# Score products as 32x64 array tiles, and ninety small products in TensorE's warm-up

## The chip, the core and the metric

One core of one Trainium2 chip runs the whole program. The metric is the device time of one execution in microseconds (us); the median of three runs is compared. [...]

## The reference, cut to what matters

Three parts run one after another: a chunked linear attention with decay (4 batches, 8 heads, 768 positions, head size 32, state size 16), a gated feed-forward (width 256 to 1024 to 256), and a second feed-forward (256 to 2048 to 256). Only the attention's scores are touched by the change:

```python
L = np.exp(cum[:, :, :, None] - cum[:, :, None, :]) * causal
CB = np.einsum('bhin,bhjn->bhij', Cc, Bc)          # the scores
M = CB * L
y_intra = np.einsum('bhij,bhjd->bhid', M, xc)
y_inter = np.einsum('bhin,bhnd->bhid', Cc, state) * decay_to_i[:, :, :, None]
state = decay_full[:, :, None, None] * state + np.sum(Bx, axis=2)
...
k = np.maximum(xk @ w_k, 0.0); v = k * k @ w_v     # first feed-forward, gated by a sigmoid
...
g = h - np.tanh(h); out = g @ w_out                # second feed-forward
```

## The kernel before, in words

The attention works in 12 groups of 256 tokens (`NG`), three to a batch; a group has four chunks of 64 tokens (`NC4`, `L`), and all eight heads lie in the 128 partitions, 32 partitions (two heads of 16 states) to a quarter. For group k TensorE computes:

- `decays(k)`, pd: the exponents of the decay matrix, two 128x128 products (L427 for the first two groups, in f32; L431 later, in f32r);
- `scores(k)`, pcb (L475): for each chunk, both halves `jh` of its 64 keys and four quarters q, one f32 product with 32 partitions in, 32 out and 128 columns. That is 32 products in the program; the trace has each f32 product as two weight loads and two matmuls, so 64 of each;
- `inter(k)`, py (L485): 32 products (24 for a batch's first group) of 32 in, 32 out, 64 columns; `terms(k)`, py (L500): the state's increments; `intra(k)`, py (L507): 32 products with 64 in, 32 out.

`visit_a(j)` issues `scores(j+1)` and then `inter(j)`; `visit_b(j)` issues `terms(j+1)` and `intra(j)`. pc (L405, and L676 for group 0) is the sum that ScalarE turns into the scales `er`. The first feed-forward is written as pk, pr and acc products (L771 to L774, L781 to L783): six 512-column products to a half tile; the second as ph and acc products of the same lines.

The order of each engine's instructions comes in two parts. The prologue is the list `START`, written out by hand: a name stands for a piece of work, and `qz` clears the operand `quiet`, `wa` is a number of idle 128x128x512 bf16 products on it that only keep TensorE busy (L218), `ps` is the group-0 scales' product (L676), `d0`, `d1` the first decays, `p0` `scores(0)`, `v0` the whole first visit. `wa` stands ahead of all else on TensorE. The dictionary `fns` also has entries `wb`, `wc`, `wd`, which `START` does not name. All that follows is ordered by `Plan.run`, a list scheduler in the program text that gives each piece a planned cost (P is TensorE, A ScalarE, V VectorE) and picks the next by rank and planned start. So a changed cost in one call of `put` can move pieces on every engine. Engines work strictly in this order.

Of the kernel before, what the change touches and what calls it, by code (L numbers as in the profile page):

```python
# [16 lines left out]
P = 128  # L17
NB, NH, S, HD, NS = 4, 8, 768, 32, 16
NQ = NH // 2
L = 64  # L20
# [6 lines left out]
NC4 = GT // L  # L27
NGB = S // GT
NG = NTOK // GT
# [28 lines left out]


START = """  # L60
    qz tab Da Dla Dca Db0 Dx0 Db1 Dx1 W Db2 Dnk Dnr seg mk wa c0t c1t c0b st mk2 tri
    cA lA cC lC sA ss h0s x0a cD lD x0b ps pe d0 e0 dec dexp still heads c1b x1a x1b sD cum p0 s0 w0 m0 ob u0 h0 w1
    r0t r0b r1t r1b spread v0 d1 e1 pr0 nu
""".split()
# [6 lines left out]
def t_act(n, more=0.0):  # L71
    return 0.172 + n / 1200 + more
# [124 lines left out]
def chain_kernel(ctx, tc, xb, a, an, a0, bc, mu_k, mu_r, w_k, w_v, w_r, w_in, w_out, out):  # L197
    nc = tc.nc
    V, A, G, PE = nc.vector, nc.scalar, nc.gpsimd, nc.tensor
# [15 lines left out]
    def fill(n):  # L215

        for _ in range(n):
            PE.matmul(acc[:, 0], quiet, quiet.unsqueeze(1).to_broadcast([P, NC4, P]), start=True, stop=True)  # L218

    def bank(name, shape=(2, BLK)):  # L220
        return pairs.tile([P, *shape], F32, tag="pair", name=name)


    acc = accp.tile([P, 2, BLK], F32, name="acc")
# [14 lines left out]
    quiet = const.tile([P, P], BF16, name="quiet")  # L239
# [134 lines left out]
    xbt, bct, cp, bp, mt, sts, er = {}, {}, {}, {}, {}, {}, {}  # L374
# [9 lines left out]
    def apart(k):  # L384
        return bct[k][:, GT:].rearrange("p (e c i) -> p e c i", e=2, c=NC4)
# [73 lines left out]
    def quarter(q):  # L459
        return slice(32 * q, 32 * q + 32)  # L460

    def half(h):
        return slice(L * h, L * h + L)

    QUADS = [(q, q >> 1, q & 1) for q in range(4)]

    def scores(k):
        pcb = pcbs[k] = bank("pcb")
        pv = pcb.rearrange("p g (e c i) -> p g e c i", e=2, c=NC4)
        for c in range(NC4):  # L470
            for jh in range(2):
                o = L * c + 32 * jh
                for q, h2, hp in QUADS:
                    r = quarter(q)
                    PE.matmul(pv[quarter(2 * h2 + jh), hp, :, c], bct[k][r, o:o + 32], apart(k)[r, :, c], start=c == 0, stop=c == NC4 - 1, skip_group_check=True)  # L475

    def out_bank(k):
        pys[k] = bank("py")

    def inter(k):  # L480
        for c in range(0 if k % NGB else 1, NC4):
            for e in range(2):
                for q, h2, hp in QUADS:
                    r, o = quarter(q), quarter(2 * hp + e)
                    PE.matmul(  # L485
                        pys[k][o, h2 ^ hp, c * L:(c + 1) * L], sts[k][r, c, e * HD:(e + 1) * HD], cp[k][r, e, c * L:(c + 1) * L],
                        start=first(k, h2 ^ hp, 2 * hp + e), stop=False, skip_group_check=True,
                    )
# [28 lines left out]
    def visit_a(k):  # L517
        if k + 1 < NG:
            scores(k + 1)
        out_bank(k)  # L520
        inter(k)
# [32 lines left out]
    def prologue(fetch1):  # L554

        t0, t1, t2, t3, t4 = vec("f"), vec("h"), vec("s"), vec("l", F32R), vec("f")
        seg, one = t0[:, 0, 0:GT], t0[:, 1, 0:P]
        la, ca = t4[:, 0, 0:NU], t4[:NC, 1, 0:GT]
        tri, cf = t1[:, 0, 0:P], t3[:NC, :, 0:GT]
        ad, mk = t2[CUM:P, 0, 0:GT], t2[:, 1]  # L560
# [4 lines left out]
        st = early["st"] = held[:, 0, 0:GT].rearrange("p (k h j) -> p k h j", k=2, h=2)  # L565
# [4 lines left out]
        def warm(n):  # L570
            return lambda: fill(n)

        def load(t, v):
            return lambda: nc.sync.dma_start(out=t, in_=v)
# [33 lines left out]
        def causal(out, e):  # L608
            return lambda: copy(e, out[0:L], mk[0:L, 0:L].unsqueeze(1).to_broadcast([L, CQ, L]))
# [71 lines left out]
        def t_nu():  # L681
# [4 lines left out]
            G.memset(xall[:, :, 0:NB * (S + 1)].rearrange("p c (b s) -> p c b s", b=NB)[..., 0:1], 0.0)  # L686

        fns = dict(
            qz=lambda: V.memset(quiet, 0.0), wa=warm(8), wb=warm(3), wc=warm(2), wd=warm(2), seg=t_seg,
            mk=t_mk, mk2=t_mk2, st=t_st, tri=t_tri, still=t_still, heads=t_heads, spread=t_spread,  # L690
            tab=lambda: A.preload_act_table_set("natural_log_exp_and_others"),
            c0t=causal(by[0], "V"), c1t=causal(by[1], "V"), c0b=spread(by[0], CUM, TOK, soon, "A"), c1b=spread(by[1], CUM, TOK, soon, "A"),
# [3 lines left out]
            Da=load(ad, a0), Dla=load(la, a), Dca=load(ca, an), Dnk=load(mus["k"], mu_k), Dnr=load(mus["r"], mu_r), W=fetch1,  # L696
            Db0=lambda: bc_load(0), Db1=lambda: bc_load(1), Db2=lambda: bc_load(2), Dx0=lambda: xb_load(0), Dx1=lambda: xb_load(1),
# [12 lines left out]
    def attention():  # L710

        D, E, MK, CH, GS, BPt, X, XL, BL, PSX, PS = ({} for _ in range(11))
        users = []

        def put(*args, **kw):
            t = add(*args, **kw)
            users.append(t)
            return t

        def at(k):  # L720
            return RANK_T * k

        def scales(b, lo, rank, after):
            take = [(R["pair"], ("pc", b))] + ([(R["er"], b)] if b else [])
            p = put(dict(P=0.36), lambda e: scales_sum(b, lo), after, rank, take)
            PSX[b] = put(dict(A=t_act(S - lo)), lambda e: scales_exp(b, lo), [p], rank, uses=[take[0], (R["er"], b)], func="exp")
            return p

        PS[0] = scales(0, 2 * GT, at(2) - 2, [])
        X[0] = put(dict(A=t_act(BLK), V=t_dve(BLK)), lambda e: group_out(0, e), [], at(0), (), [(R["pair"], ("py", 0))])  # L730
        first_half = visited = None
        for k in range(1, NG + 1):
            if 2 <= k < NG:
                XL[k] = put(dict(S=0.47), lambda e, k=k: xb_load(k), [], at(k - 1.5), [(R["xb"], k)], dma=1.7)
                if k >= 3:
                    BL[k] = put(dict(S=0.47), lambda e, k=k: bc_load(k), [], at(k - 1.8), [(R["bc"], k)], dma=1.7)
                rw = put(dict(S=0.9), lambda e, k=k: rows(k), [], at(k - 1.2), [(R["rows"], k)], dma=0.2)
                D[k] = put(dict(P=0.47), lambda e, k=k: decays(k), [rw], at(k) - 1.5, [(R["pair"], ("pd", k)), (R["L"], k)], [(R["rows"], k)])
                E[k] = put(dict(A=t_act(1024)), lambda e, k=k: decays_exp(k), [D[k]], at(k) - 1.5, (), [(R["pair"], ("pd", k)), (R["L"], k)], func="exp")
                BPt[k] = put(dict(V=t_dve(GT)), lambda e, k=k: weigh(k), [XL[k]], at(k) - 1.5, [(R["bp"], k)], [(R["xb"], k)], port=True)  # L740
            b, g = divmod(k, NGB)
            if g == 0 and k < NG:
                pr = put(dict(S=0.45), lambda e, b=b: prep_rows(b), [PS.get(b - 2)], at(k - 1.2), (), dma=0.2)
                PS[b] = scales(b, 0, at(k) - 1.7, [pr])
            if k >= 2:
                j = k - 1
                take = ([(R["pair"], ("pcb", k))] if k < NG else []) + [(R["pair"], ("py", j))]
                use_a = [(R["cp"], j), (R["state"], j), (R["bc"], k)]
                use_b = [(R["pair"], ("py", j)), (R["L"], j), (R["xb"], j), (R["bp"], k), (R["xb"], k)]
                first_half = put(dict(P=1.85 if k < NG else 0.85), lambda e, j=j: visit_a(j), [CH[j], GS[j], BL.get(k), D.get(k), PS.get(b) if k < NG else None, MK[j]], at(j), take, use_a)  # L750
                pause = put(dict(X=PAUSE), lambda e: None, [first_half])
                visited = put(dict(P=1.25 if k < NG else 0.75), lambda e, j=j: visit_b(j), [pause, XL.get(j), XL.get(k), BPt.get(k)], at(j), (), use_b)
                X[j] = put(dict(A=t_act(BLK), V=t_dve(BLK)), lambda e, j=j: group_out(j, e), [visited], at(j), (), [(R["pair"], ("py", j))])
            if k == NG:
                break
            MK[k] = put(dict(V=t_dve(1024)), lambda e, k=k: mask(k), [first_half, E.get(k)], at(k), (), [(R["pair"], ("pcb", k)), (R["L"], k)])
            CH[k] = put(
                dict(V=0.29 * moves(k)), lambda e, k=k: chain(k), [visited, PSX[b] if k > 1 else None], at(k) - 0.5,
                ([] if g else [(R["state"], k)]) + ([(R["state"], k + 1)] if g < NGB - 1 else []),
                [(R["pair"], ("py", k - 1)), (R["er"], b)] + ([(R["state"], k)] if g else []), port=True,  # L760
            )
            GS[k] = put(dict(V=t_dve(BLK)), lambda e, k=k: group_scale(k), [BL.get(k), PSX[b] if k > 1 else None], at(k) - 0.5, [(R["cp"], k)], [(R["bc"], k), (R["er"], b)], port=True)
        return X, users
# [258 lines left out]
    with tc.manual_schedule():  # L1022
# [9 lines left out]
        k0, k1, v0, k2, r, v1, k3, v2, v3 = done  # L1032
# [89 lines left out]
```

## Time and profile before

| | |
|---|---|
| median of 3 runs | 500.32 us (499.49 to 501.25) |
| the profiled execution | 501.04 us, its span 499.3 us |
| TensorE busy | 478.1 us, 96% of the span |
| VectorE, ScalarE busy | 399.1 us (80%), 296.4 us (59%) |
| mean granted clock of TensorE | 0.978 |
| the chain that ended last | TensorE 71%, VectorE 16%, ScalarE 7%, "issue" 3%, DMA 2% |

The span is 1.7 us shorter than the execution's own time. "Issue" is time in which an engine waited for nothing that the profile shows. A matmul's busy time includes the pipeline, so that two that follow each other overlap.

### The profile page before, as it was taken

What the parts mean: (1) busy time and instruction counts of PE and PEld (TensorE: products, weight loads), DVE (VectorE), ACT (ScalarE), POOL (GpSimd) and SP (SyncE); (2) the same over time, 40 slices, a digit from 0 to 9 for tenths busy, and PEclk for the clock granted to TensorE, in tenths of its full rate; (3) what the DMA queues carried; (4) which work ended last, traced back from release to release, by engine and by line L of the source; (5) the groups of instructions that cost most, each with busy time, mean ns of one, the idle gap of its engine ahead of it and who ended that gap; (6) DMA issues with size and microseconds to landing.
All of it is one profiled execution on the core that took longest, in us unless ns stands there. A gap on an engine that the chain in (4) does not pass through costs nothing.

```text
span 499.3 us, 10243 instructions
## 1 busy us (share of the span) xinstructions
PE 478.1 (96%) x4449; PEld 381.9 (76%) x4449; DVE 399.1 (80%) x501; ACT 296.4 (59%) x377; POOL 10.3 (2%) x29
## 2 busy tenths in 40 slices
PE   7787999999999999999999999999999999999993
PEld 3466777887778878887788788888878888887882
DVE  5588999999759999995878869668876966887681
ACT  4665987774847767665555553654555365455551
POOL 8000000000000000000000000000000000000000
PEclk9858999999999999999999999999999999999998
DMA  7565445211022212210000100000010000001001
GB/s 236 182 170 179 142 156 174 87 46 36 1 84 88 75 52 86 83 44 0 1 0 0 43 0 1 34 10 1 0 43 0 1 28 15 0 0 43 0 2 48
DMA packets 14123, 27.37 MB, mean 55 GB/s; under 512 B 2256, under 2 KB 3152, under 8 KB 14072
## 3 DMA queue, kind: packets, MB, share of 16 engines
q1 hardware_dynamic: 14072, 26.65, 16.8%
q8 instruction: 37, 0.61, 0.5%
q14 instruction: 14, 0.11, 0.1%
HBM read 23.30 MB, written 3.34 MB: 53 GB/s over the span
## 4 chain that ended last, share of the span: by engine, by line
PE 71%; DVE 16%; ACT 7%; issue 3%; DMA 2%; POOL 1%; POOLq 0%; DVEq 0%; ACTq 0%
PE acc L781 10%; PE acc L783 10%; PE acc L782 10%; PE ph L772 8%; PE ph L771 8%; PE ph L774 8%; PE pk L771 3%; PE pk L772 2%; PE pk L774 2%; DVE l L804 2%; PE pcb L475 2%; PE py L485 2%; DVE f L905 2%; DVE f L909 2%; PE py L507 1%
## 5 line engine op out<-in xcount | busy, mean ns | idle before, releaser
L900 ACT ACTIVATE s<-ph 128x1024 f32<-128x1024 f32 (+1 forms) x49 | 49.5, 1010 | 68.5 <-PE ph L774 68.5
L905 DVE SCALAR_TENSOR_TENSOR f<-f,s 128x1024 f32<-128x1024 f32 (+1 forms) x49 | 58.8, 1200 | 30.2 <-ACT f L901 30.0
L353 ACT ACTIVATE h<-f 128x1024 fp32r<-128x1024 f32 (+1 forms) x43 | 44.8, 1041 | 50.7 <-DVE f L909 47.8
L771 PE MATMUL ph<-xh,winh 128*128 128x512 f32 x192 | 74.7, 389 | 0.0
L772 PE MATMUL ph<-xh,winl 128*128 128x512 f32 x192 | 74.7, 389 | 0.0
L781 PE MATMUL acc<-h,wouth 128*128 128x512 f32 x188 | 73.6, 391 | 0.3
L918 DVE TENSOR_TENSOR l<-f,h 128x1024 fp32r<-128x1024 f32 (+1 forms) x49 | 58.9, 1201 | 18.6 <-ACT h L353 18.0
L783 PE MATMUL acc<-l,wouth 128*128 128x512 f32 x188 | 73.4, 391 | 0.3 <-DVE l L918 0.2
L782 PE MATMUL acc<-h,woutl 128*128 128x512 f32 x188 | 73.2, 389 | 0.0
L909 DVE TENSOR_TENSOR f<-ph,f 128x1024 f32<-128x1024 f32 (+1 forms) x49 | 58.8, 1201 | 3.3
L774 PE MATMUL ph<-xl,winh 128*128 128x512 f32 x192 | 59.1, 389 | 0.0
L901 ACT ACTIVATE f<-s,biases 128x1024 f32<-128x1024 f32 (+1 forms) x49 | 55.7, 1137 | 1.6
L781 PEld LDWEIGHTS acc<-h,wouth 128*128 128x128 f32 x188 | 35.3, 188 | 9.1 <-ACT f L901 1.5
L772 PEld LDWEIGHTS ph<-xh,winl 128*128 128x128 f32 x192 | 36.0, 188 | 7.5
L771 PEld LDWEIGHTS ph<-xh,winh 128*128 128x128 f32 x192 | 36.0, 188 | 7.5
L774 PEld LDWEIGHTS ph<-xl,winh 128*128 128x128 f32 x192 | 36.0, 188 | 7.5
L783 PEld LDWEIGHTS acc<-l,wouth 128*128 128x128 f32 x188 | 35.3, 188 | 8.5 <-DVE l L918 1.1
L782 PEld LDWEIGHTS acc<-h,woutl 128*128 128x128 f32 x188 | 35.3, 188 | 7.2
L771 PE MATMUL pk<-xh,wkh 128*128 128x512 f32 x96 | 39.3, 409 | 0.6 <-issue 0.5
L781 PE MATMUL acc<-h,wvh 128*128 128x512 f32 x96 | 38.4, 400 | 0.8 <-DVE xall L833 0.8
L772 PE MATMUL pk<-xh,wkl 128*128 128x512 f32 x96 | 38.0, 396 | 0.0
L783 PE MATMUL acc<-l,wvh 128*128 128x512 f32 x96 | 37.6, 391 | 0.0
(135 smaller groups left out, 760.1 us busy)
## 6 DMA issues: line engine op xcount, KB each, us to landing
bct<-in_bc SPq DMA_DIRECT2D x12, 384.0 KB, 3.1
xbt<-in_xb SPq DMA_DIRECT2D x12, 384.0 KB, 3.6
raw<-in_w_in SPq DMA_DIRECT2D x8, 512.0 KB, 4.4
raw<-in_w_out SPq DMA_DIRECT2D x8, 512.0 KB, 3.6
out<-ob SPq DMA_DIRECT2D x11, 256.0 KB, 2.2
raw<-in_w_k SPq DMA_DIRECT2D x4, 512.0 KB, 7.3
raw<-in_w_v SPq DMA_DIRECT2D x4, 512.0 KB, 3.9
raw<-in_w_r SPq DMA_DIRECT2D x1, 512.0 KB
```

Of the source, the lines that this page charges most:

```text
L353: A.activation(out=out, in_=in_, func=AF.Copy)
L771: PE.matmul(o, wh[:, k, ms], hi[:, k], start=k == 0, stop=False)
L772: PE.matmul(o, wl[:, k, ms], hi[:, k], start=False, stop=False)
L774: PE.matmul(o, wh[:, k, ms], lo[:, k], start=False, stop=k == 1)
L781: PE.matmul(acc[:, c], wh[:, k, cs], h[:, e], start=first, stop=False, skip_group_check=True)
L782: PE.matmul(acc[:, c], wl[:, k, cs], h[:, e], start=False, stop=False, skip_group_check=True)
L783: PE.matmul(acc[:, c], wh[:, k, cs], l[:, e], start=False, stop=last, skip_group_check=True)
L900: A.activation(out=s, in_=phs[j, i][:, e], func=AF.Square, accum_out=sums[:, c:c + 1])
L901: A.activation(out=qs[j, i][:, e], in_=s, func=AF.Square, scale=PA, bias=pbias)
L905: V.scalar_tensor_tensor(out=q, in0=q, scalar=PG, in1=s, op0=ALU.add, op1=ALU.mult)
L909: V.tensor_tensor(out=q, in0=phs[j, i][:, e], in1=q, op=ALU.mult)
L918: V.tensor_tensor(out=l[:, e], in0=qs[j, i][:, e], in1=f(h[:, e]), op=ALU.subtract)
```

## The change

```diff
 START = """
-    qz tab Da Dla Dca Db0 Dx0 Db1 Dx1 W Db2 Dnk Dnr seg mk wa c0t c1t c0b st mk2 tri
+    qz tab Da Dla Dca Db0 Dx0 Db1 Dx1 W Db2 Dnk Dnr seg mk wa ws wb c0t c1t c0b st mk2 tri
...
+    def small(n):
+
+        for _ in range(n):
+            PE.matmul(acc[0:32, 0, 0:32], quiet[0:32, 0:32], quiet[0:32, 0:32], start=True, stop=True)
...
         for c in range(NC4):
-            for jh in range(2):
-                o = L * c + 32 * jh
-                for q, h2, hp in QUADS:
-                    r = quarter(q)
-                    PE.matmul(pv[quarter(2 * h2 + jh), hp, :, c], bct[k][r, o:o + 32], apart(k)[r, :, c], start=c == 0, stop=c == NC4 - 1, skip_group_check=True)
+            for q, h2, hp in QUADS:
+                r = quarter(q)
+                PE.matmul(pv[half(h2), hp, :, c], bct[k][r, L * c:L * (c + 1)], apart(k)[r, :, c], start=c == 0, stop=c == NC4 - 1, skip_group_check=True)
...
-            qz=lambda: V.memset(quiet, 0.0), wa=warm(8), wb=warm(3), wc=warm(2), wd=warm(2), seg=t_seg,
+            qz=lambda: V.memset(quiet, 0.0), wa=warm(2), ws=lambda: small(90), wb=warm(7), wc=warm(2), wd=warm(2), seg=t_seg,
...
-                first_half = put(dict(P=1.85 if k < NG else 0.85), lambda e, j=j: visit_a(j), ...
+                first_half = put(dict(P=1.6 if k < NG else 0.85), lambda e, j=j: visit_a(j), ...
```

A score product now takes all 64 keys of a chunk at once (32 partitions in, 64 out), 16 products to a group in place of 32. The warm-up is two wide products, ninety of 32x32x32, and seven wide ones, in place of eight wide ones. The planned cost of `visit_a` is 1.6 in place of 1.85.

On TensorE's queue at its start, the warm-up and what follows it. Before (`quiet` is the cleared operand):

```order
L218 LDWEIGHTS quiet
L218 MATMUL acc<-quiet 128x512
L676 MATMUL pc<-xl 128x256 x2
L427 MATMUL pd<-xh,xl 128x512 x2
L667 MATMUL acc<-f,h 128x192
L475 MATMUL pcb<-bct 32x2x64 x32
L500 MATMUL py<-xbt,bp 32x64 x16
```

The first two rows stand eight times. After:

```order
L223 LDWEIGHTS quiet
L223 MATMUL acc<-quiet 32x32
L218 LDWEIGHTS quiet
L218 MATMUL acc<-quiet 128x512
...
L679 MATMUL pc<-xl 128x256 x2
L432 MATMUL pd<-xh,xl 128x512 x2
L670 MATMUL acc<-f,h 128x192
L478 MATMUL pcb<-bct 64x2x64 x16
L503 MATMUL py<-xbt,bp 32x64 x16
```

Two wide products stand ahead of these rows, the small one stands ninety times and the wide one behind it seven times: 91 matmuls and 91 weight loads more stand ahead of the first scales, and each group's scores have half the products.

On TensorE's queue where the first feed-forward begins, the products pk behind the third visit's end. Before:

```order
L500 MATMUL py<-xbt,bp 32x64 x16
L507 MATMUL py<-L,xbt 32x64 x32
L431 MATMUL pd<-rr,sr 128x512 x2
L475 MATMUL pcb<-bct 32x2x64 x32
L485 MATMUL py<-cp,st 32x64 x24
L771 MATMUL pk<-xh,wkh 128x512
L772 MATMUL pk<-xh,wkl 128x512
...
L774 MATMUL pk<-xl,wkh 128x512 x2
```

After:

```order
L503 MATMUL py<-xbt,bp 32x64 x16
L510 MATMUL py<-L,xbt 32x64 x32
L774 MATMUL pk<-xh,wkh 128x512
L775 MATMUL pk<-xh,wkl 128x512
...
L777 MATMUL pk<-xl,wkh 128x512 x2
L436 MATMUL pd<-rr,sr 128x512 x2
...
L478 MATMUL pcb<-bct 64x2x64 x16
L488 MATMUL py<-cp,st 32x64 x24
```

The first half of pk's first tile now stands ahead of the decays, its second half ahead of the scores; before, both stood behind the scores and `inter`. From here to the end of the attention the scheduler interleaves the same pieces in another order on TensorE, VectorE, ScalarE and the DMA queue; the second feed-forward keeps its order.

## Rows read from the trace of the kernel before

**Rows 1.** The page: busy time of TensorE (PE), its weight loads, VectorE (DVE), ScalarE (ACT).

```profile
PE 478.1 (96%) x4449; PEld 381.9 (76%) x4449; DVE 399.1 (80%) x501; ACT 296.4 (59%) x377; POOL 10.3 (2%) x29
q8 instruction: 37, 0.61, 0.5%
```

**Rows 2.** Busy time by stage: us, engines with instruction counts, granted clock, DMA share, GB/s.

```profile
60.00:75.00 15.00, 14.99 (x379) 11.57 (x377) 13.92 (x28) 12.68 (x16) 0.00 (x0) 1.00 0.52 177
75.00:100.00 25.00, 24.45 (x399) 19.83 (x399) 24.82 (x40) 19.15 (x25) 0.00 (x0) 1.00 0.42 130
100.00:125.00 25.00, 25.00 (x513) 20.11 (x512) 24.07 (x37) 15.56 (x19) 0.00 (x0) 1.00 0.14 41
```

**Rows 3.** The chain that ended last, to 45 us: start, us, piece.

```profile
6.17 2.07 PE pc L676 x4
...
12.60 1.31 PE pcb L475 x64
...
16.40 1.80 issue
...
41.79 1.84 issue
```

**Rows 4.** Timeline of TensorE and its weight loads, start: start, us, engine, line, products, idle before.

```profile
1.09 3.60 PE L218 MATMUL acc<-quiet 128*128 128x512 bf16 x8 [1.09 <-DVE quiet L689]
6.17 2.07 PE L676 MATMUL pc<-xl 32*128 32x256 f32 x4 [1.49 <-ACT xl L353]
...
9.19 0.34 PEld L427 LDWEIGHTS pd<-xh,xl 128*128 128x128 f32 x1 [0.52 <-issue]
10.04 0.34 PEld L427 LDWEIGHTS pd<-xh,xl 128*128 128x128 f32 x1 [0.52 <-issue]
...
26.87 0.33 PE L485 MATMUL py<-cp,st 32*32 32x64 f32 x2
...
26.95 1.24 PE L485 MATMUL py<-cp,st 32*32 32x64 f32 x58
```

**Rows 5.** From the start to the first and the third "issue" wait: the counts.

```profile
0.00:17.30 17.30, 13.82 (x222) 7.07 (x222) 10.58 (x29) 10.18 (x15) 10.26 (x29) 1.00 0.64 199
...
0.00:42.70 42.70, 33.43 (x856) 20.21 (x857) 29.77 (x65) 26.42 (x40) 10.26 (x29) 0.84 0.66 201
```

**Rows 6.** Timeline of TensorE around one scores-and-inter block, 65 to 70 us.

```profile
65.52 1.14 PE L475 MATMUL pcb<-bct 32*32 32x128 f32 x63
66.39 0.24 PE L485 MATMUL py<-cp,st 32*32 32x64 f32 x1
...
66.40 0.90 PE L485 MATMUL py<-cp,st 32*32 32x64 f32 x63
67.24 0.50 PE L781 MATMUL acc<-h,wvh 128*128 128x512 f32 x1
...
69.36 0.57 PE L500 MATMUL py<-xbt,bp 64*32 64x64 f32 x25
```

**Rows 7.** Line L475 in two neighbouring stretches: matmuls in flight; then its durations (ns).

```profile
65.51:65.64 0.13, 0.12 (x8) 1.00 1.13 441
65.64:65.75 0.11, 0.11 (x16) 1.00 0.95 372
L475 PE MATMUL pcb<-bct x768: 267/268/418, 12.5 to 133.3; 32*32 32x128 f32 x192
```

**Rows 8.** A slow stretch of the start: the granted clock is the column behind POOL.

```profile
27.00:36.00 9.00, 7.29 (x256) 5.67 (x237) 7.49 (x15) 4.48 (x8) 0.00 (x0) 0.50 0.73 216
```

**Rows 9.** Timeline where pk begins: its operands xh and xl, and its first product.

```profile
39.98 1.05 ACT L353 ACTIVATE xh<-f 128x1024 fp32r<-128x1024 f32 x1
41.22 1.22 DVE L804 TENSOR_TENSOR xl<-f,xh 128x1024 fp32r<-128x1024 f32 x1
...
44.21 0.80 PE L771 MATMUL pk<-xh,wkh 128*128 128x512 f32 x1
```

More of the change, by code (lines that the diff above doesn't have):

```diff
@@ L749, in attention @@
                 use_b = [(R["pair"], ("py", j)), (R["L"], j), (R["xb"], j), (R["bp"], k), (R["xb"], k)]
-                first_half = put(dict(P=1.85 if k < NG else 0.85), lambda e, j=j: visit_a(j), [CH[j], GS[j], BL.get(k), D.get(k), PS.get(b) if k < NG else None, MK[j]], at(j), take, use_a)
+                first_half = put(dict(P=1.6 if k < NG else 0.85), lambda e, j=j: visit_a(j), [CH[j], GS[j], BL.get(k), D.get(k), PS.get(b) if k < NG else None, MK[j]], at(j), take, use_a)
                 pause = put(dict(X=PAUSE), lambda e: None, [first_half])
```

## The prediction

> **What bounds the kernel now.** Views in this order: the page for the busy shares, the stages, then the chain of the first 45 us, then the timeline of one score block. TensorE is busy 96% of the span [rows 1]. After the start it leaves hardly a gap: 64.4 of the 65 us from 60 to 125, at the full clock [rows 2]. So time taken off TensorE there should come off the end. VectorE is a close second: 62.8 of 65 us busy in the same stages [rows 2], so it can follow a TensorE that becomes faster by about 2 us there and not by more.
>
> The first 44 us are another matter. The chain runs through TensorE from 6.17 us, when the first scales' operand is ready, through pc (2.07), pd and acc to `scores(0)` at 12.60 [rows 3], 6.43 us. All of that is at 1.2 GHz: the loads of pd start 0.85 us apart, for two passes over 512 columns [rows 4], whatever the clock column says before its first recorded change. Later stretches show 0.50 in that column too [rows 8]. And three times TensorE stands still for 1.7 to 1.8 us with no releaser ("issue") [rows 3]. Those waits are instruction fetches. TensorE ran 444 instructions (matmuls and loads) before the first wait and 1713 before the third [rows 5], so 1269 apart: five times 256, within the few that a stretch's end cuts off. [...] The products of the attention are used up faster than the next 256 arrive; the long feed-forward products are not.
>
> [...]
>
> **The scores.** In a saturated block the 64 score matmuls start in rounds of eight: eight in flight in the first stretch of 0.13, sixteen one stretch of 0.11 later, each 0.267 long [rows 7]. Eight rounds of 0.109 are 0.87, and `inter` starts 0.88 behind the first [rows 6]. A round is eight tiles, four quarters of the partitions by two column tiles. The new form makes rounds of four tiles, each as wide as two of the old, with the same 128 columns to stream: again eight rounds. So the scores themselves stay at 0.87. What is halved is the supply: the trace shows 58 `inter` matmuls in 1.24 us, 0.33 of it the length of the last: 16 ns a matmul with its load [rows 4]. Scores and `inter` are 128 such pairs, 2.1 us of supply, of which a part was queued ahead behind the long products; the block took 67.24 - 65.52 = 1.72 [rows 6]. With 96 pairs the supply is 1.56, 0.54 less, and the array is the limit: 0.87 for the scores and, since 64 columns take half a round's 128, 8 x 0.055 = 0.44 for `inter`. Now its last matmul starts at 66.40 + 0.90 - 0.24 = 67.06, 0.18 before the next product [rows 6]; that stays: 0.87 + 0.44 + 0.18 = 1.49. Saved: 0.23 a block, between 0 (a 64-wide weight load that slows each round by a third of its 0.11) and 0.54. Seven such blocks lie behind 44 us, two of them with a wait for VectorE inside, where I count nothing: **5 x 0.23 = 1.15 us** (0 to 3.8).
>
> **The start behind the warm-up.** Before `scores(0)` 182 instructions are added (91 products, 91 loads), and each group's scores go from 128 to 64, so the crossings move. Counting the new order in steps of 256 from the first: it falls 54 earlier in `inter(0)`; its fetch starts before `scores(1)` and no longer in it, so its end comes some 0.9 us sooner and 0.5 of work lies behind it: -0.4. The second falls inside the decays of group 1, with 0.4 us of small products and two 0.85 us products as cover: between 0 and 1.2 lost, +0.5. The third stays where it is. The fourth, so far in scores at the slow clock, falls into `inter(2)`: 0 to 1.8, +0.5. The one that cost 1.84 at 41.79 moves behind pk products, which cover it: TensorE can then start pk when xh is there, at 41.0, and not at 44.21 [rows 9], but it waits there for xl (42.4) in order, so I count -1.5 of the 1.84. Shorter score blocks in groups 2 and 3: -0.5. Sum **-1.4 us** (-3.3 to +1.5).
>
> **The warm-up.** It grows by one wide product (8 in 3.60, so 0.43 to 0.45 [rows 4]) and ninety small ones. No row has their price. A wide product takes 0.43 for 512 columns, so 32 columns are 27 ns at that clock. Below, the supply gives 16 ns; above, half a score round, 0.055, a load and 64 columns in two passes at the full clock. I take 27, since each must stream 32 columns through one tile and its load can run under the product before it: 90 x 0.027 = 2.4. Two changes of tile shape, 0.1 each (the 0.18 above, of which part is length). The warm-up ends at 1.09 + 0.85 + 2.4 + 0.2 + 3.0 = 7.5 in place of 4.7, and the idle 1.49 us before the first scales [rows 4] hide only half of that: pc starts **1.35 us later**. Nothing else on the prologue's path waits less.
>
> What it buys is the clock. pc, pd and acc together are 6.43 us at 1.2 GHz [rows 3], 3.2 at 2.4. In the run shown the rise fell within `scores(0)` (its longest matmul 418 ns, the others 267 [rows 7]), behind full-width products since 8.2. There the eight wide products ended at 4.7 and the engine then idled; now seven of them run from 4.5 straight into the first scales. How soon that raises the clock no row tells. The bounds: at 6, within the last wide products, or no sooner than now. At 6 the 1.5 us of wide products that are left take 0.75, pc starts at 6.8 and `scores(0)` at 10.0, 2.6 sooner than at 12.60; in the other case 1.3 later. I take the middle, a rise at 9.3 within pc: 1.8 of the 6.43 run slow, the rest in half the time, and `scores(0)` starts at 7.5 + 1.8 + 2.3 = 11.6, **1.0 us sooner** (+1.3 to -2.6).
>
> **Sum.** -1.15 - 1.4 - 1.0 = -3.55 us. The profiled execution took 501.04 (span 499.3), so 497.5 by its own time; the median shown is 0.7 less than that execution, which makes the forecast **496.8**.
>
> **Rivals.** (1) *Late clock.* 32-partition products such as pc ran from 6.17 to 8.24 without a rise, and a single 32x32 tile uses less of the array still. Then -1.15 - 1.4 + 1.3 = -1.25: 499.1. (2) *Small products count in full.* Then TensorE is without a gap from 1.09 and the rise comes before the first scales; the last wide ones take half their time too and `scores(0)` starts about 2.6 us sooner: -5.15, 495.2. Against it stands pc, dense and without a rise [rows 3, 7]. [...] (3) *Slower:* small products cost 55 ns each, not 27, and the clock stays low. The place is the wait before pc, the price 90 x 0.028 = 2.5 more: -1.25 + 2.5 = +1.25, 501.6. It is a loss from 41 ns a product on (90 x 0.014 = 1.25). For it: loads and products alternate on one tile. Against: `terms` does so on four tiles, and 25 of its matmuls with their loads take 0.57, 0.24 of it the length of one [rows 6], so each tile takes a load and 64 columns in two passes every 0.055. (4) *The change of tiles does nothing, and the new order gives the rest back:* rounds are the limit before and after, and the stages where VectorE is 97% busy [rows 2] set the pace; the early gain is lost when pk, now ahead of the scores, waits for xl. Then about 0: 500.
>
> **How the numbers follow.** Forecast 0.38, (1) 0.28, (2) 0.12, (3) 0.08, (4) 0.14. This kernel's runs tell about 0.3% (1.5 us) from no change. Faster: forecast and (2), half of (1): 0.64. Same: the other half and most of (4): 0.25. Slower: (3) and the unlucky end of (4): 0.11. The range leaves out the far ends of (2) and (3): 494.3 to 500.9; the forecast's own range is 495.5 to 498.5.
>
> **What would show it.** The profile after should have: small products 27 ns apart and pc starting near 7.5; pd's loads 0.43 apart rather than 0.85 (the clock); score blocks of about 1.5 in place of 1.72, with `inter` still starting 0.87 behind the scores; an "issue" wait in `inter(0)` again, none where pk begins; at most a few tenths more gaps on TensorE between 60 and 150 us. The prediction is wrong if pc starts beyond 9, if a score round takes over 0.12, or if TensorE shows waits for VectorE where it had none.

## The result, and the profile after

| | median | all runs | ratio to before, 95% interval |
|---|---|---|---|
| before, beside the changed kernel | 498.06 us | 495.66 to 501.25 (20) | |
| changed kernel | **501.48 us** | 499.06 to 505.66 (20) | 1.0069, 1.0045 to 1.0092 |

The change makes the kernel slower by 3.4 us. The prediction was 3.5 us faster than the 500.32 it started from; its range of 494.3 to 500.9 does not hold the time, and the sign is wrong. The starting point was the median of three runs; over 20 runs the kernel before is 2.3 us below it, at 498.06.

The two profiled executions don't show this difference: that of before took 501.04 us, 3.0 more than the median of its 20 runs, and that of the changed kernel 500.42, 1.1 less than its own. So the places are read from the profiles and the sizes from the medians. The page after, beside [rows 1]:

```profile
span 498.7 us, 9662 instructions
PE 476.0 (95%) x4156; PEld 381.0 (76%) x4156; DVE 397.3 (80%) x501; ACT 298.4 (60%) x377; POOL 10.3 (2%) x29
q8 instruction: 34, 0.56, 0.4%
```

TensorE has fewer instructions, as it should, and three packets of instructions fewer. Its timeline from the start, beside [rows 3, 4] (start, us, engine, line, count, idle before):

```profile
1.09 1.03 PE L218 MATMUL acc<-quiet 128*128 128x512 bf16 x2 [1.09 <-DVE quiet L692]
2.06 2.58 PE L223 MATMUL acc<-quiet 32*32 32x32 bf16 x90
4.57 2.95 PE L218 MATMUL acc<-quiet 128*128 128x512 bf16 x7
7.45 1.12 PE L679 MATMUL pc<-xl 32*128 32x256 f32 x4
8.51 1.98 PE L432 MATMUL pd<-xh,xl 128*128 128x512 f32 x4
10.33 0.49 PE L670 MATMUL acc<-f,h 128*128 128x192 f32 x2
10.74 1.10 PE L478 MATMUL pcb<-bct 32*64 32x128 f32 x32
12.35 0.65 PE L503 MATMUL py<-xbt,bp 64*32 64x64 f32 x32 [0.50 <-DVE bp L451]
...
18.89 1.55 PE L432 MATMUL pd<-xh,xl 128*128 128x512 f32 x3 [2.62 <-issue]
```

Ninety small products take 2.5 us, 28 ns each; pc starts at 7.45, takes 1.12 and not 2.07, and `scores(0)` starts at 10.74 and not 12.60 (12.53 by the timeline). So in this execution the clock was up when the real work began (the record has its rise at 7.2). But `terms(0)` then waits 0.50 for VectorE's bp, and in d1 a fetch, a wait without a releaser (what the traces show of these stands under **Fetches**), takes 2.62.

A new wait stands behind the third visit. All engines there in the changed kernel, beside [rows 9]:

```profile
35.12 0.32 PE L510 MATMUL py<-L,xbt 64*32 64x64 f32 x9 [1.18 <-issue]
...
35.50 0.60 ACT L358 ACTIVATE xall<-py 128x512 f32<-128x512 f32 x1 [0.36 <-PE py L510]
36.00 1.05 ACT L358 ACTIVATE xh<-f 128x1024 fp32r<-128x1024 f32 x1
...
36.40 0.92 DVE L551 SCALAR_TENSOR_TENSOR st<-st,er,py 128x64 f32<-128x64 f32 x3
...
37.42 0.19 PEld L774 LDWEIGHTS pk<-xh,wkh 128*128 128x128 f32 x1 [2.15 <-ACT xh L358]
37.46 0.47 PE L774 MATMUL pk<-xh,wkh 128*128 128x512 f32 x1 [2.02 <-DVE st L551]
37.49 0.82 ACT L413 ACTIVATE er<-pc 128x768 f32<-128x768 f32 x1
...
38.36 1.22 DVE L534 TENSOR_TENSOR L<-pcb,L 128x1024 f32<-128x1024 f32 x1
```

pk now follows `intra(2)` directly. When `intra(2)` ends, ScalarE copies its result (xall<-py, 0.60) and only then makes xh (1.05, ready at 37.05); VectorE updates the state from the same py (to 37.32). TensorE, with nothing else in its queue ahead of pk, stands still for 2.0 us. What ends the wait is the state update, and not xh, which is ready 0.27 earlier: where TensorE plainly waits for ScalarE, as at 65.88 below, it starts 0.05 behind it. By the program pk, py, pcb, pc and pd share three buffers (`pairs`, `bufs=3`); at 37.4 pcb has still to be read at 38.36 and pc at 37.49, so the buffer that pk can take is that of py, once VectorE has read it. That last step is read from the program and the order of the rows; no run tests it alone.

Before, the decays, `scores(4)` and `inter(3)` lay in between: `intra(2)` ends at 39.4 in the profile of before, xh is ready at 41.03, and pk's turn comes behind them [rows 9]. There TensorE stands still for 0.28 and then for the fetch of 1.84:

```profile
41.45 0.34 PE L485 MATMUL py<-cp,st 32*32 32x64 f32 x15 [0.28 <-DVE st L548]
43.63 0.66 PE L485 MATMUL py<-cp,st 32*32 32x64 f32 x33 [1.84 <-issue]
```

So between `intra(2)` and pk the idle time is about the same in both profiles, 2.12 and 2.02. Nor does the chain that ended last go through pk in the changed kernel. It follows the copy and the state updates and stays on VectorE to 42 us, with waits for a transfer and for ScalarE further on (start, us, piece):

```profile
35.50 0.61 ACT xall L358
37.31 1.14 DVE xl L807
38.45 1.14 DVE L L534
...
51.40 4.42 DMA raw<-in_w_k
```

The waits of TensorE by cause, after (line waited for, cause: us in total, times, longest):

```profile
PE pd L432 <- issue: 2.6, 1, 2.6
PE py L510 <- issue: 2.5, 2, 1.3
PE pk L774 <- DVE st L551: 2.0, 1, 2.0
...
PE py L488 <- ACT L L447: 1.2, 1, 1.2
```

The last is a second wait of the new order: an `inter` at 65.88 waits 1.23 for ScalarE's exponential of decays (L), which comes after two table loads of 1.28.

### The profile page after: what moved, and what is told of

It reads as the page before. It is cut to its first block, busy times and chain, and to the rows that moved or that the text cites. A ratio compares the mean times of both kernels' runs of the same rounds, so it can differ in the third digit from the quotient of the medians.

```text
span 498.7 us, 9662 instructions
## 1 busy us (share of the span) xinstructions
PE 476.0 (95%) x4156; PEld 381.0 (76%) x4156; DVE 397.3 (80%) x501; ACT 298.4 (60%) x377; POOL 10.3 (2%) x29
## 4 chain that ended last, share of the span: by engine, by line
PE 67%; DVE 19%; ACT 7%; DMA 3%; issue 2%; DVEq 0%; SPq 0%; ACTq 0%
PE acc L784 10%; PE acc L786 9%; PE acc L785 9%; PE ph L777 8%; PE ph L775 8%; PE ph L774 8%; DVE l L807 3%; DMA raw<-in_w_in 2%; PE pk L774 2%; PE pk L775 2%; PE pk L777 2%; DVE f L908 2%; PE py L510 2%; DVE f L912 2%; PE py L488 1%
## 5 line engine op out<-in xcount | busy, mean ns | idle before, releaser
L358 ACT ACTIVATE h<-f 128x1024 fp32r<-128x1024 f32 (+1 forms) x44 | 45.8, 1040 | 51.2 <-DVE f L912 48.1
```

The source lines that it names most:

```text
L358: A.activation(out=out, in_=in_, func=AF.Copy)
```

## The experiments

Each kernel was timed beside the kernel before (498.2 to 498.8 us in these comparisons). Names of pieces are those of the kernel's description.

**The parts one by one.** `scores_only`, `plan_only` and `warmup_only` take one of the three edits of the diff each, `scores_warmup` the two without the cost:

```diff
+ scores_only:   pv[half(h2), hp, :, c], bct[k][r, L * c:L * (c + 1)]   (16 products of 32x64)
+ plan_only:     put(dict(P=1.6 if k < NG else 0.85), ... visit_a(j)
+ warmup_only:   wa=warm(2), ws=lambda: small(90), wb=warm(7)
+ scores_warmup: the first and the third
```

> Only the score products are 32x64; warm-up and planned cost are those of before, so the order of the pieces is that of before. Theory A (the loss is in the new order): 0 to 2 us faster than before, since instructions fall away and nothing moves. Theory B (the wider tile costs more than the products it saves): slower by 1 to 2 us, as each of some ten score-and-inter blocks takes 1.82 in place of 1.72 us and the instruction fetches fall elsewhere. Theory C (the warm-up loses it): no change, within 1 us.

> Only the planned cost of visit_a is 1.6 in place of 1.85; the same instructions in another order from the third visit on. Theory A: slower by 2 to 4 us, with TensorE waiting about 2 us for xl where the first feed-forward begins. Theory B and C: within 1 us of before.

> Only the warm-up is changed: 2 wide, 90 small, 7 wide. Theory A and B: 0 to 2 us faster, since the clock rises near 7 us and scores(0) starts near 11 in place of 12.6. Theory C: slower by 1 to 3 us, because the first scales start 1.3 us later and what is gained behind them is lost at the next instruction fetches.

> Scores 32x64 and the new warm-up, but the planned cost 1.85, so the order of before. Theory A: faster than before by 1 to 3 us. Theory B: slower by 1 to 2 us. Theory C: slower by 1 to 3 us.

| | median | ratio, 95% interval |
|---|---|---|
| scores_only | 495.63 us | 0.9922, 0.9893 to 0.9952 |
| plan_only | 504.52 us | 1.0092, 1.0057 to 1.0128 |
| warmup_only | 499.61 us | 0.9989, 0.9956 to 1.0022 |
| scores_warmup | 497.45 us | 0.9974, 0.9943 to 1.0006 |

The new order alone costs 0.9%. The scores alone gain 0.8%. The warm-up alone does nothing that can be measured. plan_only has the same wait where pk begins:

```profile
39.33 0.60 ACT L353 ACTIVATE xall<-py 128x512 f32<-128x512 f32 x1 [4.32 <-PE py L507]
39.82 1.05 ACT L353 ACTIVATE xh<-f 128x1024 fp32r<-128x1024 f32 x1
...
41.28 0.77 PE L771 MATMUL pk<-xh,wkh 128*128 128x512 f32 x1 [1.99 <-DVE st L548]
```

**Is it pk's place?** Two kernels divide the order at the third visit. `plan_early` is the kernel before with the lower cost up to visit 3 only, which moves pk ahead; `all_late` is the changed kernel with the lower cost from visit 4 only, which leaves pk behind `inter(3)`:

```diff
+ plan_early: put(dict(P=(1.6 if j <= 3 else 1.85) if k < NG else 0.85), ...
+ all_late:   put(dict(P=(1.6 if j > 3 else 1.85) if k < NG else 0.85), ...
```

> The kernel before with the planned cost 1.6 for the first four visits only (j <= 3), 1.85 afterwards: pk begins ahead of the decays, as in the changed kernel. Theory A: slower by 3 to 5 us, like the cost 1.6 everywhere. If the order further on is to blame: within 1 us of before.

> The changed kernel, but the planned cost 1.6 only from the fifth visit on (j > 3); for the first four it stays 1.85, so pk begins behind scores(4) and inter(3) as before, and the rest follows from that. If the loss comes from pk being put ahead of the decays and scores there (theory A): as fast as scores and warm-up with the old cost, about 0.997 of before, 3 to 4 us below the changed kernel, without the 2.0 us wait of pk. If it comes from the order further on: still about 1.005 to 1.009.

plan_early: 505.66 us, 1.0121 (1.0068 to 1.0173). all_late: 497.56 us, 0.9992 (0.9956 to 1.0028). Putting pk ahead costs on the kernel before, and leaving it behind takes the loss out of the changed kernel: 1.0069 against 0.9992, intervals apart. What is divided here is the scheduler's choice at the third visit with all that follows from it: by their traces, TensorE, VectorE and ScalarE of both kernels also do the later pieces of the attention in another order than the kernels that they are compared with. No run has pk's place alone changed. In all_late TensorE goes on without a wait, and xh (ready at 36.17) is there when pk's turn comes; ScalarE and TensorE:

```profile
33.89 1.22 PE L436 MATMUL pd<-rr,sr 116*128 116x512 f32 x2
34.62 0.60 ACT L358 ACTIVATE xall<-py 128x512 f32<-128x512 f32 x1
35.04 1.99 PE L478 MATMUL pcb<-bct 32*64 32x128 f32 x32
35.10 1.07 ACT L358 ACTIVATE xh<-f 128x1024 fp32r<-128x1024 f32 x1
...
36.95 0.97 PE L488 MATMUL py<-cp,st 32*32 32x64 f32 x48
...
37.85 0.59 PE L774 MATMUL pk<-xh,wkh 128*128 128x512 f32 x1
```

The rest of the attention is fuller too. The stage from 60 to 145 us in the changed kernel and in all_late, whose attention ends 5 us earlier (length, then busy time of TensorE, its loads, VectorE, ScalarE, GpSimd, clock, DMA share, GB/s):

```profile
60.00:145.00 85.00, 82.03 (x1491) 64.38 (x1490) 70.03 (x112) 59.40 (x70) 0.00 (x0) 1.00 0.26 78
```

```profile
60.00:145.00 85.00, 84.32 (x1441) 66.49 (x1425) 73.59 (x114) 59.67 (x73) 0.00 (x0) 1.00 0.25 80
```

From the end of `intra(2)` to the end of the last `intra` the changed kernel takes 107.9 us (35.4 to 143.4) and all_late 104.3 (34.0 to 138.2); TensorE's idle time in that stage is 5.0 and 1.4 us. The difference of 3.7 is the idle time: the wait at pk of 2.0, one for the exponential of 1.2 and one for a fetch of 1.3 that all_late does not have, less 0.9 of short waits that only all_late has. This is one profile of each kernel.

**The warm-up.** `wide12_scores` is scores_only with twelve wide products; `small50_behind` is the kernel before with fifty small ones in the idle time behind its eight wide ones:

```diff
+ wide12_scores:  wa=warm(12)          (START as before)
+ small50_behind: wa=warm(8), ws=lambda: small(50)
```

> Scores 32x64, planned cost 1.85, and a warm-up of twelve wide products (1.09 + 12 x 0.43 = 6.2, just when the first scales are ready) without small ones. If unbroken full-width work from 1.09 raises the clock and small products do less: rise between 4 and 8 us, pc starting at 6.2, scores(0) at about 10, and 1 to 3 us below scores 32x64 alone (0.992 of before), so 0.986 to 0.990. If the start of the chain is not what sets the end, because the instruction fetches set the pace up to 40 us: about 0.992.

> The kernel before with fifty small products behind the eight wide ones (1.4 us, in the idle time before the first scales): nothing is later, but 100 more instructions stand ahead of the first scales. Theory of the fetches: TensorE's waits without releaser stay at the counts 449 + 256 k (matmuls and loads run before), so each falls 100 instructions earlier in the program: the first no longer at the end of inter(0) but at the end of scores(1). If they were tied to the work instead, they would stay in inter(0), terms(2) and inter(3). Time: within 1.5 us of before by the fetches alone; if small products hold the clock as well as wide ones, 1 to 3 us faster.

wide12_scores: 495.11 us, 0.9932 (0.9904 to 0.9959). small50_behind: 499.72 us, 1.0017 (0.9980 to 1.0055). Neither differs from the same kernel with eight wide products. In wide12_scores the clock's rise is recorded at 4.1 and `scores(0)` starts at 9.36, three us sooner than in scores_only (12.42). `terms(0)` then waits for VectorE:

```profile
10.23 2.04 POOL L619 TENSOR_TENSOR xh<-s 32x512 f32<-32x512 f32 x2
10.48 2.07 DVE L446 TENSOR_TENSOR bp<-xbt,dec 128x256 f32<-128x256 f32 x1 [1.70 <-ACT dec L668]
...
12.60 0.59 PE L498 MATMUL py<-xbt,bp 64*32 64x64 f32 x28 [2.14 <-DVE bp L446]
```

**Combinations.** `scores_plan` (scores and cost, old warm-up), `scores_late` (scores, lower cost from visit 4), `wide12_late` (that with twelve wide products) and `wide12_late_dve` (that with the piece beside bp taken from GpSimd to VectorE):

```diff
- x1a=moving(1, 0, G), x1b=moving(1, 1, G)
+ x1a=moving(1, 0), x1b=moving(1, 1)
```

> Scores 32x64 and the planned cost 1.6 everywhere, with the warm-up of before. If pk ahead of the decays and scores costs about 0.9 per cent whatever the scores and the warm-up are: 0.992 + 0.009 to 0.012, so 1.000 to 1.004. If its price came from the 32x32 scores or the fetches at their places alone: near 0.992.

> Scores 32x64, the warm-up of before, the planned cost 1.6 from the fifth visit on only; pk stays behind scores(4) and inter(3). If only pk's place matters: 0.990 to 0.994, like scores 32x64 alone. If the order further on costs too: above 0.996.

> As scores_late, with a warm-up of twelve wide products. If the start is worth something once pk's place is right: below scores_late by 1 us or more. If terms(0) waits for bp on VectorE until about 12.5 us whatever the clock, as with twelve wide products before: within 1 us of scores_late.

> As wide12_late, with the two products of the group-1 exponents (x1a, x1b) on VectorE in place of GpSimd. In the run with twelve wide products bp took 2.07 us on VectorE, beside 2.04 us of GpSimd products, and 0.43 elsewhere. If the two engines share a way to the memory there: bp takes 0.43 again, terms(0) starts about 1.5 us sooner (near 11 us when the clock rose early), and the time falls by 0 to 1.5 us. If bp was long for another reason: it stays at 2 us.

| | median | ratio, 95% interval |
|---|---|---|
| scores_plan | 499.19 us | 0.9997, 0.9969 to 1.0025 |
| scores_late | 497.33 us | 0.9982, 0.9952 to 1.0012 |
| wide12_late | 496.26 us | 0.9949, 0.9923 to 0.9976 |
| wide12_late_dve | 496.15 us | 0.9945, 0.9919 to 0.9971 |

With the 32x64 scores the cost also takes back what they gain (0.9922 to 0.9997). Here the two halves of the order can't be told apart: scores_late has pk behind and still lies at 0.9982. So the choice at the third visit is the larger part of the loss where it was divided, and not proved to be all of it everywhere. In wide12_late_dve bp takes 0.42 and `terms(0)` starts 1.75 us sooner than in wide12_late (12.72):

```profile
10.49 0.42 DVE L446 TENSOR_TENSOR bp<-xbt,dec 128x256 f32<-128x256 f32 x1 [0.20 <-ACT dec L668]
...
10.97 0.65 PE L498 MATMUL py<-xbt,bp 64*32 64x64 f32 x32 [0.50 <-DVE bp L446]
```

Yet the time is that of wide12_late. An earlier start is not an earlier end here.

**Late or small?** The new warm-up costs nothing that can be measured on the kernel before, and 0.5% on top of the scores, where the two intervals overlap. `wide15_scores` ends its warm-up late without small products, `small45_scores` has small products and ends before pc's operand is ready:

```diff
+ wide15_scores:  wa=warm(15)
+ small45_scores: wa=warm(2), ws=lambda: small(45), wb=warm(6)
```

> Scores as 32x64 tiles, the cost of the visit left at 1.85, and fifteen wide products as warm-up: they end near 7.5 us, as late as the warm-up with the ninety small ones, with 14 instructions added and not 182. Lateness theory: the first scales start 1.35 us later than in the kernel with the narrow scores alone, and that is what the new warm-up costs; 497.5 (ratio to the kernel before 0.997). Theory of the small products (their instructions move the fetch waits, or they leave the clock low): without them nothing is lost, since the clock rises during the wide ones; 495.3 (0.993), as with twelve wide ones.

> Scores as 32x64 tiles, the cost left at 1.85, warm-up of two wide, 45 small and six wide products, which end near 5.8 us, ahead of the first scales' operand at 6.17: small products without lateness. Lateness theory: nothing is lost, 495.3 (ratio to the kernel before 0.993). Theory of the small products: the 90 instructions of them move the fetch waits into other work and leave the clock to rise later than behind wide products; 497 to 498 (0.997).

wide15_scores: 495.79 us, 0.9941 (0.9916 to 0.9966). small45_scores: 494.60 us, 0.9921 (0.9890 to 0.9952). Neither theory holds as it was put. wide15_scores was not as late as meant, since its clock rises at 4.0 and the fifteen products take 4.81 us, where 0.43 each would be 6.4: pc starts at 6.16. So lateness was not tested. And forty-five small products cost nothing that can be measured. With ninety the start differs from profile to profile; in that of scores_warmup the clock's rise is recorded at 13.4:

```profile
7.67 2.07 PE L679 MATMUL pc<-xl 32*128 32x256 f32 x4
9.67 3.78 PE L432 MATMUL pd<-xh,xl 128*128 128x512 f32 x4
...
13.74 1.10 PE L478 MATMUL pcb<-bct 32*64 32x128 f32 x32
```

The four profiles with ninety have the rise at 7.2, 7.3, 12.3 and 13.4, and `scores(0)` at 10.7, 10.8, 13.2 and 13.7. The one with 45 has it at 6.0, the four with twelve or fifteen wide products at 4.0, 4.0, 4.1 and 5.9, and `scores(0)` at 9.4 or 9.5 in all five. But scores_only, with eight wide products and 0.9922, has the rise at 13.3 and `scores(0)` at 12.4. So the clock's rise does not explain the 0.5%, and its cause stays open.

No kernel here beats scores_only, small45_scores and wide12_scores, which lie within each other's intervals at 0.992 to 0.993: the 32x64 scores with the old order are faster than both kernels of the change.

## Why the prediction was wrong

Its total can be followed through four kernels, each with one part more: scores -0.78%, the warm-up on top +0.52 (0.9974/0.9922), the order from visit 4 on +0.18 (0.9992/0.9974), pk ahead +0.77 (1.0069/0.9992); in us -3.9, +2.6, +0.9, +3.8. Only the first and last are well clear of their intervals, and the last holds the order behind pk as well as pk's place.

**The step that failed** stands in the part on the start: the wait at 41.79 "moves behind pk products, which cover it: TensorE can then start pk when xh is there", counted as **-1.5 of the 1.84**. Its first half came true: that fetch, due when 1729 instructions have been issued, falls at 47.2 in the changed kernel and costs nothing. (The fetch before it, at 1473, is in `intra(2)` in both kernels and grew from 0.47 to 1.18.) The second half failed. pk's move was booked as a gain, with xh's start of 39.98 taken from a trace [rows 9] in which three other pieces of TensorE's work ran meanwhile. With pk ahead nothing else of TensorE's stands between `intra(2)` and pk, and both xh and the state update, which ends the wait, stand behind the copy that `intra(2)` releases: 2.0 us of waiting in every kernel with pk ahead (1.99 to 2.02 in four), as much as the fetch and the short wait took before. That takes the gain back. The loss beyond it comes with the order that follows from the choice: 5.0 us of TensorE's idle time to the end of the attention against 1.4 with pk behind. Measured, the step with what follows from it is +3.8; how much of that is pk's wait alone, no run separates. Rival (4) named the place and put it down to xl, with a price that only took back the gain; by the trace xl is not what pk waits for.

**The scores: -1.15.** The rounds were right: 32 matmuls start in 1.10 - 0.27 = 0.83, four to a round, 0.11 a round. The block was not. In scores_only:

```profile
61.55 1.10 PE L473 MATMUL pcb<-bct 32*64 32x128 f32 x32
62.58 0.85 PE L483 MATMUL py<-cp,st 32*32 32x64 f32 x64
63.36 0.50 PE L779 MATMUL acc<-h,wvh 128*128 128x512 f32 x1
```

The first `inter` starts 1.03 behind the first score and not 0.87, and the block takes 1.81 where 1.49 was forecast and 1.72 stood before. The records have the last score start at 62.382 and `inter` at 62.579, a pause of 0.20 in all five blocks without another wait; before, where both are 32x32, there is none [rows 6]. The prediction had two changes of tile shape in the warm-up and none in the block; what makes the pause is not shown. So the saturated blocks lose up to 0.1 each, and the 0.23 that each was to save is not there. The gain of the 32x64 scores lies before 44 us: from the end of `intra(2)` to the end of the last `intra` scores_only takes 105.6 us and before 105.4. The last wait for a fetch ahead of pk comes there when 1473 instructions have been issued, before at 1729: one block less in the stretch where fetches are waited for. But the clock differs too: in the first 44 us the granted clock was 0.50 for 13.7 us after its first rise in the profile of before, and for 3.4 us in that of scores_only. How much of the 3.9 us is the fetch and how much the clock of single runs, no experiment separated.

**The warm-up: -1.0.** What the prediction writes as 1.2 GHz is its estimate from 2 x 512 columns in 0.85 us, and 2.4 is twice that; the traces show a granted share of 0.50 or 1.00, and pd's loads 0.85 us apart ahead of the recorded rise [rows 4] and 0.43 behind it in the changed kernel. The half of the time held: pd took 1.98 us for 3.78. 28 ns a small product (27 forecast) and pc at 7.45 (7.5 forecast) were right; the forecast rise at 9.3 lies between the 7.2 and 13.4 of the runs. What falls away is the worth of an earlier `scores(0)`: `terms(0)` is caught by bp, which isn't ready before 12.3 to 12.7 unless GpSimd's piece is moved. And the 1.75 us that bp then gives back brought nothing in the median, though in the one profile pk starts at 37.4 and not at 40.4; why not, is open. Rival (3)'s 55 ns is refuted. Rival (2) has the rise before the first scales: it came so in two of four profiles with ninety, only at the very end of the wide ones, and five to six us later in the other two, though TensorE had no gap from 1.09 on. With twelve or fifteen wide products it came at 4.0 to 5.9, with eight wide ones and a gap behind them anywhere from 3.9 to 13.3. So the runs do not tell what the small products count for.

**The other crossings.** A crossing is here the end of a step of 256 of TensorE's instructions. Forecast: first -0.4, second +0.5 (0 to 1.2). Measured: the first is hidden, the second costs 2.62, outside its bounds; the fourth (+0.5), at 31.6, is hidden too. The count of steps of 256 put both in the right place; the price taken for the second, with other work as cover, was too low: the block's first instruction started at 14.08, and the next block's at 18.89. The prediction's counts, 444 and 1713, leave out TensorE's semaphore instructions; with them they are 449 and 1729, five times 256 apart without a rest. Of the signs to look for, "at most a few tenths more gaps" from 60 to 150 us failed: 3.0 us against 0.8. And the 418 ns of [rows 7] were not in `scores(0)` alone: 102 of the 768 took over 300 ns, 64 of them between 27 and 36 us.

## What to carry to other kernels

Before a piece is counted as moved up, list what releases it in the new order, its output buffer included, and what released that: an operand that was early beside other work is late when that work goes behind. Price a tile shape by its borders too: here the shape that halved the instructions paid a pause of 0.20 where the other shape followed. When a scheduler's cost is changed, compare the whole order behind it and not the first piece that moved. And where the start is paced by instruction fetches and late operands, measure parts alone; three us gained at 10 us showed no measurable gain at the end.

## What the runs showed of the hardware

**Fetches.** In every kernel the long waits without a releaser fall, within one or two, when 193 + 256 k of TensorE's instructions have been issued, counted with the semaphore instructions of its sequencer: 449, 961, 1473, 1729 and 3265 before, 705, 1473 and 2753 after. Adding instructions moves them into other work. The traces of before and after also have the packets of the instruction queue (q8) [rows 1], 16,384 bytes each: one lands 1.2 to 1.6 us ahead of the end of each of these waits (before at 16.58, 29.91, 37.41, 42.15 and 74.24, after at 17.44, 33.88 and 69.53). Such a wait is called a fetch here. From the first instruction of one block to the first of the next at such a wait it took 4.8 us at the 2.62 after and 4.9 at the 1.84 before, but 3.2 to 8.4 over all kernels: no fixed delay fits, and what sets it stays open. In small45_scores the wait of 2.15 us for VectorE lies inside the first block, and all that is left of waiting for fetches is 0.26 us; it has the lowest median of all, though its ratio (0.9921) is that of scores_only (0.9922):

```profile
PE py L503 <- DVE bp L451: 2.1, 1, 2.1
...
PE py L510 <- issue: 0.3, 1, 0.3
```

Most crossings show no wait. Before, of the seven up to 1729 instructions, in the first 42 us, three cost 1.7 to 1.8 us and one 0.47; of the 28 behind them one costs 0.55.

**VectorE beside GpSimd.** bp took 2.07 us in wide12_scores while GpSimd worked on its own two-operand piece (two products, 2.04), and 0.42 in wide12_late_dve without it. The runs show this much; what the two engines share is not shown.

**The clock** of the first 45 us rises and falls back at other times in kernels with the same start: behind eight wide products the first rise is recorded at 3.9, 4.5, 4.6 or 12.5 to 13.3. The runs of one kernel spread by some 0.5% on either side (before: 495.66 to 501.25). The one explains the other only in small part: over the 104 runs of the kernel before beside the experiments, a lower mean granted clock goes with a longer time only weakly (correlation -0.41, about a sixth of the variance). What makes the rest of the spread is open.
